# Turning attention scores over in 32x32 blocks on VectorE instead of by products with the identity on TensorE

## The chip, the cores and the metric

The kernel runs on one core of one Trainium2 chip. The metric is the device time of one execution in microseconds (us). Engines are named as the profile names them: PE is TensorE's matrix products, PEld its weight loads, DVE is VectorE, ACT is ScalarE, POOL is GpSimd, and SP issues the transfers (DMA).

## What is computed

Eight batches, each with eight heads, of 512 tokens and 32 state rows, 64 numbers a head, go through two softmaxes over one matrix of scores, and all rows then go through a feed-forward layer with a rational function between its two products:

```
scores = scale * np.matmul(x, state.transpose(0, 1, 3, 2))
a      = softmax over the last axis (the 32 state rows)
xread  = np.matmul(a, state)
scores2 = scale * np.matmul(state, x.transpose(0, 1, 3, 2))
a2     = softmax over the last axis (the 512 tokens)
sread  = np.matmul(a2, x)
h = concat(xread, sread) @ w_in
P = a0 + a1*h + a2*h^2 + a3*h^3
Q = 1 + |b0|*|h| + |b1|*h^2
out = (P / (Q + 1e-6)) @ w_out
```

`scores2` is `scores` transposed, so one set of products gives both. The weights are 512x2048 and 2048x512; they arrive as 64-bit numbers, and the kernel itself makes 32-bit ones of them.

## The kernel before, in words

**Front and back.** The work is 72 steps: batch b (0 to 7) has steps 8b to 8b+7, one for each eighth of the 2048 inner columns, and steps 64 to 71 do the same for the rows of `sread`. Step n begins with a *front* (`F:n:0` and `F:n:1`, line 687): 12 products of 128x512 that give 1024 columns of h in PSUM. xread is not formed: the state rows are multiplied with w_in once at the start (`X:i`, line 606, copied out by `XA:i` at line 618 and stored to DRAM) and the front multiplies that product (tile m) with the softmax weights (tile aT), both split into a high and a low part. ACT and DVE then make the rational function of h: ACT copies and logarithm and exponential (lines 699 to 802), DVE six operations of 128x1024 (`mu`, `po`, `qd`, `g1`, `g2`, `g3` at lines 710, 714, 720, 731, 737, 743), POOL the low part `gl` (line 750). The *back* (`mh:n:t` four products, `ml:n:t` two, line 760) multiplies them with w_out into four PSUM banks, one for each 128 tokens.

**Softmax of a batch.** It is done beside the steps of the batch ahead. `scores:b` (line 404) puts the scores into PSUM as ps_sc: partition 32k+s is state row s of head pair k, 2x512 columns are tokens. ACT copies them to sT (`sc_copy`). `row_T` turns sT over by eight 128x128 products with the identity (line 434, function `transposes`) into ps_s; DVE takes the maximum of each group of 32 (`row_max`, line 458) and subtracts it (`row_sub`, line 466), both from PSUM, into e1; ACT takes the exponential, DVE the sum, POOL multiplies with its reciprocal (`row_norm`, line 507). `a_T` turns e1 back by eight more products into ps_a; ACT takes its high part (`a_hi`, line 517), DVE the low part (`a_lo`, line 521). These are aT, which the fronts of the batch read. The other softmax runs along the columns of sT; its weights e2 are turned over by eight products of the same kind (`e2_T`).

**Buffers.** Four PSUM banks hold the outputs (o0 to o3), the other four are two buffers of the tag "h", which fronts, the products X and, from batch 1 on, ps_sc, ps_s, ps_a, ps_e and ps_sr take in turns. Batch 0 uses the output banks for its softmax.

**Order.** The program is a written list of 2266 operations (`ORDER`); each engine does its own instructions in the list's order and waits at each until its inputs are there and its output's buffer is free. SP issues all transfers in the list's order as well.

Of the kernel before, what the change touches and what calls it, by code (L numbers as in the profile page):

```python
# [18 lines left out]
P = 128  # L19
# [4 lines left out]
    "warm:8 lt:0:0 lr:0 cp:0 ls:0:2 scores:0:0 lr:1 jr:0 cp:1 jl:0 lc cb lt:0:1 scores:0:1 sc_copy:0:0 "  # L24
    "col_max:0:0 sc_copy:0:1 col_max:0:1 col_scale:0:0 lr:2 cp:2 X:0 fh:0 XA:0 col_scale:0:1 "
    "col_exp:0:1 lr:3 row_T:0:1 row_max:0:1 ls:2:8 row_sub:0:1 jw:0 XS:0 jr:1 X:3 fo:0 row_T:0:0 "
    "col_exp:0:0 X:1 row_exp:0:1 row_sum:0:1 lr:4 row_max:0:0 lr:5 XA:3 XS:3 cp:3 XA:1 row_sub:0:0 XS:1 "
    "e2_T:0:0 e2_copy:0:0 X:2 row_exp:0:0 lr:6 row_eps:0:1 row_norv:0:1 jl:1 a_T:0:1 row_sum:0:0 "
    "row_eps:0:0 a_hi:0:1 cp:4 XA:2 XS:2 e2_T:0:1 lr:7 X:5 row_norv:0:0 e2_copy:0:1 a_T:0:0 a_lo:0:1 "
    "col_eps:0 a_hi:0:0 a_lo:0:0 XA:5 XS:5 X:4 fh:1 cp:6 F:0:1 lq:0:0 fo:1 F:0:0 cp:5 jr:2 jl:2 b0a "  # L30
    "jr:3 XA:4 FC:0 lq:0:1 FB:0 qd:0 F:1:1 cp:7 F:1:0 lr:9 FB:1 FC:1 jl:3 XS:4 sp:7 sp:6 mu:0 po:0 qa:0 "
    "ln:0 qd:1 ex:0 jw:1 X:9 XA:9 lr:8 cp:8 lr:11 mu:1 po:1 lr:10 cp:10 XS:9 sread:0:0 cp:9 X:8 XA:8 "
    "XS:8 col_norm:0 jr:5 jr:4 jl:4 X:6 fh:2 fo:2 sread:0:1 sr_copy:0 g1:0 g2:0 XA:6 cp:11 lr:13 XS:6 "
    "qa:1 lr:15 sr_T:0 sr_fin:0 lr:14 jl:5 lr:12 g3:0 gl:0 X:12 fh:3 XA:12 XS:12 F:2:1 F:2:0 FC:2 FB:2 "
    "fo:3 sp:10 mh:0:0 mu:2 X:13 XA:13 XS:13 ln:1 sp:11 cp:12 qd:2 ex:1 mh:0:1 ml:0:1 cp:14 mh:0:2 "
    "ml:0:2 po:2 g1:1 g2:1 X:7 XA:7 jr:6 X:10 XA:10 ml:0:0 jr:7 cp:15 jl:7 lt:1:1 g3:1 gl:1 cp:13 qa:2 "
    "ln:2 X:11 XS:7 F:3:1 F:3:0 FB:3 FC:3 XA:11 jl:6 mh:0:3 ml:0:3 mh:1:3 ex:2 lt:1:0 scores:1:0 "
    "scores:1:1 XS:10 mu:3 qd:3 po:3 sp:14 sp:15 ml:1:3 lr:16 sc_copy:1 cp:16 lr:17 jw:4 mh:1:0 "
    "col_max:1 qa:3 lr:21 XS:11 X:17 X:14 XA:17 jw:2 jr:8 ml:1:0 g1:2 g2:2 g3:2 cp:17 ml:1:2 "
    "col_scale:1 XA:14 lr:20 X:15 XS:17 mh:1:2 row_T:1 row_max:1 row_sub:1 ln:3 mh:2:1 XS:14 jl:8 jw:3 "  # L40
    "cp:20 XA:15 XS:15 col_exp:1:0 cp:21 X:16 XA:16 lr:18 col_exp:1:1 gl:2 XS:16 lr:19 col_eps:1 fh:4 "
    "fo:4 X:18 XA:18 XS:18 row_exp:1 mh:1:1 cp:18 jr:10 jl:10 ml:1:1 X:20 fh:5 XA:20 fo:5 cp:19 F:4:1 "
    "F:4:0 FB:4 jr:9 col_norm:1 jl:9 X:21 FC:4 mh:2:2 mu:4 qd:4 sp:18 mh:2:3 XA:21 ml:2:1 sp:19 mh:2:0 "
    "lr:25 ex:3 ml:2:3 po:4 lr:22 XS:20 cp:22 g1:3 lr:23 cp:23 lr:24 cp:24 jr:12 XS:21 X:19 XA:19 XS:19 "
    "X:23 XA:23 cp:25 jr:11 jl:11 qa:4 lr:26 g2:3 g3:3 ml:2:0 sp:23 jl:12 X:22 sp:22 F:5:1 F:5:0 XS:23 "
    "FB:5 FC:5 mh:3:0 ml:2:2 mu:5 po:5 XA:22 cp:26 qd:5 lr:27 ln:4 mh:3:2 mh:3:1 XS:22 X:24 ex:4 g1:4 "
    "XA:24 XS:24 fh:6 fo:6 lm:8 mh:3:3 gl:3 lq:1:1 qa:5 ml:3:3 ml:3:0 X:26 XA:26 XS:26 ml:3:2 g2:4 g3:4 "
    "e2_T:1 e2_copy:1 row_sum:1 jr:13 cp:27 gl:4 X:25 XA:25 X:28 row_eps:1 row_norm:1:1 XS:25 jl:13 "
    "jw:7 mh:4:0 ln:5 ex:5 fh:7 F:6:1 XA:28 fo:7 g1:5 row_norm:1:0 F:6:0 FC:6 FB:6 qd:6 fs:8 ml:4:0 "
    "sp:26 ml:4:3 sp:27 XS:28 X:27 XA:27 lr:30 cp:30 ml:3:1 mu:6 po:6 qa:6 ln:6 ml:4:1 mh:4:2 lq:1:0 "  # L50
    "mh:4:3 X:30 XA:30 sread:1:0 sread:1:1 sr_copy:1 lr:28 g2:5 g3:5 gl:5 ex:6 mh:5:1 lr:31 mh:4:1 "
    "sr_T:1 sr_fin:1 cp:31 XS:27 XS:30 lr:29 X:29 XA:29 X:31 XA:31 mh:5:0 a_T:1 F:7:0 jr:15 F:7:1 jl:15 "
    "cp:28 ml:5:2 sp:31 mh:5:2 ml:5:3 g1:6 g2:6 a_hi:1 ml:4:2 a_lo:1 F:8:0 F:8:1 ml:5:1 sp:30 jr:14 "
    "cp:29 ml:5:0 FC:7 FB:7 mh:5:3 jl:14 qd:7 sp:29 sp:28 mh:6:3 mh:6:2 mu:7 po:7 mh:6:0 mh:6:1 lm:9 "
    "fs:9 FB:8 qd:8 qa:7 g3:6 F:9:1 F:9:0 gl:6 ml:6:2 ml:6:3 ln:7 ex:7 g1:7 mh:7:1 mh:7:2 FC:8 mu:8 "
    "po:8 FC:9 lm:10 ml:6:1 fs:10 FB:9 mh:7:3 F:10:1 g2:7 qa:8 ln:8 ex:8 F:10:0 g3:7 gl:7 ml:7:0 lm:11 "
    "ml:7:2 ml:7:1 qd:9 qa:9 ml:6:0 mu:9 po:9 FC:10 lm:13 lt:2:0 g1:8 FB:10 g2:8 g3:8 lt:2:1 scores:2:0 "
    "scores:2:1 mh:7:0 fl:7:2 gl:8 mu:10 po:10 qd:10 sc_copy:2 col_max:2 lq:2:1 ml:7:3 fl:7:3 mh:8:2 "
    "fl:7:1 fs:11 mh:8:3 mh:8:1 ml:8:1 ln:9 ml:8:3 ex:9 row_T:2 F:11:0 g1:9 g2:9 fl:7:0 mh:8:0 ml:8:0 "
    "mh:9:1 g3:9 row_max:2 F:11:1 mh:9:2 ml:8:2 mh:9:3 row_sub:2 qa:10 ln:10 ex:10 gl:9 ml:9:3 lm:12 "  # L60
    "ml:9:2 fs:12 F:12:0 FB:11 qd:11 qa:11 F:12:1 col_scale:2 col_exp:2:0 lm:16 g1:10 mh:10:1 ml:9:0 "
    "g2:10 g3:10 gl:10 mh:10:0 mh:9:0 FC:11 mu:11 po:11 ml:10:3 ml:10:1 fs:13 FB:12 ml:9:1 qd:12 "
    "col_exp:2:1 F:13:0 F:13:1 ln:11 ml:10:0 mh:10:2 ex:11 g1:11 mh:11:1 mh:11:3 mh:11:2 FC:12 FB:13 "
    "lq:2:0 g2:11 g3:11 FC:13 mh:10:3 gl:11 ml:11:1 mu:12 mh:11:0 po:12 lm:14 qd:13 ml:11:3 mu:13 po:13 "
    "row_exp:2 row_sum:2 qa:12 row_eps:2 e2_T:2 fd:7:1 fs:14 lm:15 fs:15 F:14:0 F:14:1 ln:12 ex:12 "
    "g1:12 mh:12:3 fd:7:2 fd:7:3 qa:13 ln:13 ex:13 mh:12:1 col_eps:2 col_norm:2 ml:11:0 ml:10:2 g2:12 "
    "g3:12 gl:12 mh:12:2 FC:14 g1:13 e2_copy:2 FB:14 qd:14 sread:2:0 sread:2:1 mh:13:1 jw:5 "
    "row_norm:2:1 sr_copy:2 sr_T:2 mu:14 row_norm:2:0 XS:29 sr_fin:2 po:14 g2:13 g3:13 mh:12:0 ml:12:0 "
    "ml:12:3 qa:14 ln:14 ex:14 lm:17 mh:13:0 g1:14 a_T:2 a_hi:2 fs:16 F:15:1 F:15:0 mh:13:2 ml:12:2 "
    "ml:11:2 a_lo:2 F:16:1 F:16:0 FC:15 ml:12:1 gl:13 ml:13:0 ml:13:3 ml:13:2 g2:14 FB:15 qd:15 mh:13:3 "  # L70
    "mu:15 po:15 mh:14:0 fd:7:0 fs:17 F:17:0 F:17:1 lt:3:0 g3:14 gl:14 qa:15 ln:15 mh:14:3 ml:13:1 "
# [860 lines left out]
```

## Time and profile before

| | |
|---|---|
| median of the runs | 690.88 us |
| lowest of the runs | 688.37 us |
| profiled execution, its own time | 690.54 us |
| its span in the trace | 688.7 us |
| busy in the span: PE, DVE, ACT, POOL | 661.9, 620.1, 524.1, 298.7 us |
| mean granted clock of TensorE | 0.987 |

A busy time is the time in which the engine had an instruction under way, also when that instruction itself was held up. Products are pipelined, so the cost of one is read from the distance of starts and not from its duration. "L434" is line 434 of the kernel before; in the changed kernel the lines behind the list stand a few numbers higher.

### The profile page before, as it was taken

Reading aid. Unit: us, or ns where it says so; the run is one execution under the profiler, and the core shown is the slowest. Engines: PE = TensorE matmul, PEld = TensorE weight load, DVE = VectorE, ACT = ScalarE, POOL = GpSimd, SP = SyncE. Lnnn points to the kernel's source line nnn. Section 1 sums busy time; section 2 is a strip of 40 time slices with the busy share of each in tenths; the row PEclk is TensorE's granted clock in tenths of the full one; section 3 lists DMA queues with packets and bytes.
Section 4 is the critical chain, followed back from the end, with each engine's and each line's share of the span. In section 5 each row is a group of like instructions: output and inputs, shape, how many; then the busy total and the mean of one; then the engine's idle time right before and its main releaser. Section 6 shows DMA issues by size and latency. Waiting matters only on the chain.

```text
span 688.7 us, 11564 instructions
## 1 busy us (share of the span) xinstructions
PE 661.9 (96%) x4602; PEld 525.3 (76%) x4602; DVE 620.1 (90%) x589; ACT 524.1 (76%) x641; POOL 298.7 (43%) x172
## 2 busy tenths in 40 slices
PE   6688889999999999999999999999999999999997
PEld 4455556778887778878887888788878788888895
DVE  4788689999999999999999999999899889998996
ACT  5889789887876876877778677777887777666773
POOL 0024146554554454434554444354444445445542
PEclk8989999999999999999999999999999999999999
DMA  7988877605122300451015022221203021300311
GB/s 290 327 298 327 304 290 277 225 37 196 64 77 92 127 17 25 125 190 39 18 60 199 15 98 72 92 82 71 78 33 137 2 75 55 99 0 33 107 47 30
DMA packets 29434, 81.49 MB, mean 118 GB/s; under 512 B 3268, under 2 KB 3396, under 8 KB 29380
## 3 DMA queue, kind: packets, MB, share of 16 engines
q1 hardware_dynamic: 29380, 80.75, 33.8%
q8 instruction: 36, 0.59, 0.4%
q14 instruction: 18, 0.15, 0.1%
HBM read 52.95 MB, written 27.79 MB: 117 GB/s over the span
## 4 chain that ended last, share of the span: by engine, by line
PE 77%; DVE 7%; DMA 6%; ACT 5%; issue 2%; POOL 1%; SPq 0%; POOLq 0%; ACTq 0%; DVEq 0%
PE h L687 25%; DMA m_dram<-xo 3%; DMA raw<-in_w_in_dram 2%; ACT xo L618 2%; PE o__3063 L760 2%; PE ps_x L606 2%; PE o__5992 L760 2%; PE o__3659 L760 2%; PE o__4266 L760 2%; PE o__3652 L760 2%; PE o__3604 L760 2%; PE o__5977 L760 2%; PE o__5430 L760 2%; PE o__3107 L760 2%; PE o__4244 L760 2%
## 5 line engine op out<-in xcount | busy, mean ns | idle before, releaser
L750 POOL TENSOR_TENSOR gl<-C,L 128x1024 fp32r<-128x1024 f32 (+1 forms) x71 | 168.9, 2379 | 271.1 <-DVE C L743 170.0
L687 PE MATMUL h<-aT,m 128*128 128x512 f32 x768 | 188.6, 392 | 0.8 <-ACT xo L618 0.8
L687 PEld LDWEIGHTS h<-aT,m 128*128 128x128 f32 x768 | 143.1, 188 | 33.1 <-ACT xo L618 2.9
L699 ACT ACTIVATE C<-h,cst 128x1024 f32<-128x1024 f32 (+1 forms) x72 | 83.1, 1156 | 40.9 <-PE h L687 33.3
L706 ACT ACTIVATE A<-h,cst 128x1024 f32<-128x1024 f32 (+1 forms) x72 | 76.9, 1068 | 47.1 <-PE h L687 41.7
L731 DVE SCALAR_TENSOR_TENSOR gh<-C,cst,L 128x1024 fp32r<-128x1024 f32 (+1 forms) x72 | 95.6, 1328 | 13.1 <-ACT L L802 9.5
L720 DVE SCALAR_TENSOR_TENSOR A<-A,b0a,h 128x1024 f32<-128x1024 f32 (+1 forms) x72 | 87.4, 1214 | 14.2 <-ACT A L706 10.4
L647 POOL TENSOR_TENSOR m<-m_sb,m 128x512 fp32r<-128x512 f32 x56 | 75.0, 1348 | 46.1 <-ACT m L646 22.0
L743 DVE SCALAR_TENSOR_TENSOR C<-C,cst,A 128x1024 f32<-128x1024 f32 (+1 forms) x72 | 91.0, 1263 | 2.1
L714 DVE SCALAR_TENSOR_TENSOR C<-C,cst,h 128x1024 f32<-128x1024 f32 (+1 forms) x72 | 87.7, 1219 | 1.9
L737 DVE SCALAR_TENSOR_TENSOR A<-A,gh 128x1024 f32<-128x1024 f32 (+1 forms) x72 | 87.5, 1216 | 1.7
L710 DVE TENSOR_TENSOR C<-C,h 128x1024 f32<-128x1024 f32 (+1 forms) x72 | 83.0, 1154 | 5.3 <-ACT C L699 2.7
L726 ACT ACTIVATE A<-A 128x1024 f32<-128x1024 f32 (+1 forms) x72 | 72.7, 1012 | 15.4 <-DVE A L720 15.4
L792 ACT ACTIVATE L<-A 128x1024 f32<-128x1024 f32 (+1 forms) x72 | 73.0, 1015 | 3.4 <-POOL gl L750 0.5
L802 ACT ACTIVATE L<-L 128x1024 f32<-128x1024 f32 (+1 forms) x72 | 73.1, 1015 | 1.8
L606 PE MATMUL ps_x<-win_sb,st 64*32 64x256 f32 x1024 | 39.6, 432 | 12.3 <-ACT xo L618 6.1
L337 POOL TENSOR_TENSOR wo<-cv_r,wo 128x512 fp32r<-128x512 f32 x16 | 23.3, 1476 | 59.8 <-ACT wo L336 59.6
L606 PEld LDWEIGHTS ps_x<-win_sb,st 64*32 64x32 f32 x1024 | 18.5, 116 | 28.1 <-issue 10.8
L646 ACT CAST m<-m_sb 128x512 fp32r<-128x512 f32 x56 | 33.9, 615 | 2.9 <-PE h L687 2.9
L618 ACT COPY xo<-ps_x 128x1024 f32<-128x1024 f32 (+1 forms) x32 | 28.8, 908 | 5.3 <-DMA m_dram<-xo 4.1
L299 ACT ACTIVATE cv_y<-raw 128x512 f32<-128x512 f32 x32 | 21.9, 695 | 11.1 <-DMA raw<-in_w_in_dram 8.7
L687 PEld LDWEIGHTS h<-sh,m 128*128 128x128 f32 x192 | 24.1, 191 | 0.6
(266 smaller groups left out, 1124.0 us busy)
## 6 DMA issues: line engine op xcount, KB each, us to landing
m_sb<-m_dram SPq DMA_DIRECT2D x56, 256.0 KB, 3.7
m_dram<-xo SPq DMA_DIRECT2D x24, 512.0 KB, 4.6
out_dram<-o_sb SPq DMA_DIRECT2D x34, 256.0 KB, 3.3
xT_sb<-in_xT_dram SPq DMA_DIRECT2D x16, 512.0 KB, 5.0
raw<-in_w_in_dram SPq DMA_DIRECT2D x16, 512.0 KB, 6.8
raw<-in_w_out_dram SPq DMA_DIRECT2D x16, 512.0 KB, 6.0
x_sb<-in_x_dram SPq DMA_DIRECT2D x16, 512.0 KB, 5.0
w_in_dram<-win_sb SPq DMA_DIRECT2D x8, 512.0 KB, 4.2
```

The costliest lines, as they stand in the source:

```text
L647: nc.gpsimd.tensor_tensor(m[:, 1], t, m[:, 0].bitcast(F32), op=ALU.subtract)
L687: nc.tensor.matmul(h[:, ci * W : (ci + 1) * W], l, r, start=(q == 0), stop=(q == len(seq) - 1),)
L699: nc.scalar.activation(e["C"], e["h"], AF.Identity, scale=cst[:, 3:4], bias=cst[:, 2:3])
L706: nc.scalar.activation(e["A"], e["h"], AF.Abs, scale=cst[:, 5:6])
L710: nc.vector.tensor_tensor(e["C"], e["C"], e["h"], op=ALU.mult)
L714: nc.vector.scalar_tensor_tensor(e["C"], e["C"], cst[:, 1:2], e["h"], op0=ALU.add, op1=ALU.mult)
L720: nc.vector.scalar_tensor_tensor(e["A"], e["A"], b0a, e["h"], op0=ALU.add, op1=ALU.mult)
L731: nc.vector.scalar_tensor_tensor(e["gh"], e["C"], cst[:, 0:1], e["L"], op0=ALU.add, op1=ALU.mult)
L737: nc.vector.scalar_tensor_tensor(e["A"], e["A"], 1.0 + 1e-6, e["gh"].bitcast(F32), op0=ALU.add, op1=ALU.mult)
L743: nc.vector.scalar_tensor_tensor(e["C"], e["C"], cst[:, 0:1], e["A"], op0=ALU.add, op1=ALU.subtract)
L750: eng.tensor_tensor(e["gl"], e["C"], e["L"], op=ALU.mult)
L760: nc.tensor.matmul(O[t], e[l][:, j * W + t * P : j * W + (t + 1) * P], wo[:, k, 2 * u + j, :], start=(place == FIRST[n // U, t] and i + j ...
```

## The change

`row_T` no longer uses TensorE: one DVE instruction turns over each 32x32 block of ps_sc on its way from PSUM to e1. A group of 32 state rows is a block's height, so each token's scores of one head again stand in 32 neighbouring columns, and `row_max` and `row_sub` work on e1 in SBUF. `a_T` is a DVE instruction of the same kind from e1 to a new tile eT, which for batches 1 to 7 lies in the buffer of e2; `a_hi` and `a_lo` read eT. `e2_T` keeps its products. `row_sub` is done by POOL in all batches (`row_sup`), `a_lo` by POOL in batches 0, 2, 3 and 4 (`a_lp`). Of the work at the start, five of the 32 copies `XA` go from ACT to DVE (`XV`) and four of the 16 weight splits from POOL to DVE (`sv`); one `row_norm` half and one 128x512 `gl` go from POOL to DVE as well. The list has the same length and is in another order throughout.

```diff
     def row_T(b, j=None):
-        transposes(b, "ps_s", 2, TS[b]["sT"], j)
+        e1 = once(b, "e1", at_tile("e1", [P, 2, S]))
+        for i in (0, 1) if b == 0 and j is None else (j,):
+            nc.vector.transpose(flat(half(e1, i)), flat(half(TS[b]["ps"], i)))
...
-            stat(mx, j), slots(TS[b]["ps_s"], j), axis=AX.X, op=ALU.max
+            stat(mx, j), slots(TS[b]["e1"], j), axis=AX.X, op=ALU.max
...
-        nc.vector.tensor_tensor(
-            slots(e1, j),
-            slots(T["ps_s"], j),
+        (eng or nc.vector).tensor_tensor(
+            e1,
+            e1,
...
     def a_T(b, j=None):
-        transposes(b, "ps_a", 2, TS[b]["e1"], j)
+        t = once(b, "eT", lambda: at.tile([P, 2, S], F32, name="eT", tag="e2" if b else "e2T"))
+        nc.vector.transpose(flat(half(t, j)), flat(half(TS[b]["e1"], j)))
...
-        nc.scalar.copy(half(AT[b][:, 0], j), half(TS[b]["ps_a"], j))
+        (copy or nc.scalar.copy)(half(AT[b][:, 0], j), half(TS[b]["eT"], j))
...
-        nc.vector.tensor_tensor(
+        (eng or nc.vector).tensor_tensor(
             half(a[:, 1], j),
-            half(TS[b]["ps_a"], j),
+            half(TS[b]["eT"], j),
...
+        "sv": lambda i: conv_split(i, nc.vector),
...
+        "a_lp": lambda b, j=None: a_lo(b, j, nc.gpsimd),
+        "row_sup": lambda b, j=None: row_sub(b, j, nc.gpsimd),
```

One line of the list on either side, out of batch 6:

```diff
-    "col_scale:6 ml:39:3 fl:39:2 FB:43 mh:40:2 ml:39:1 fl:39:0 lm:45 fl:39:3 row_T:6 mh:40:3 gl:40 "
+    "mh:41:1 FB:43 mh:41:0 g3:41 row_T:6 row_max:6 fl:39:2 fd:39:2 mh:40:2 ml:40:2 gl:41 ml:41:3 "
```

**TensorE, batch 6, between its scores and the end of its softmax.** Before (h is a front, o a back, ps_s the turned scores):

```order
L404 MATMUL ps_sc<-xT_sb,st 32x256 x16
L760 MATMUL o__3659<-wo,gl 128x512 x4
L687 MATMUL h<-aT,m 128x512 x12
L760 MATMUL o__3604<-wo,gl 128x512 x2
L760 MATMUL o__4244<-wo,gh 128x512 x4
L760 MATMUL o__3652<-wo,gl 128x512 x2
L434 MATMUL ps_s<-ident,sT 128x128 x8
L760 MATMUL o__4266<-wo,gh 128x512 x4
```

After, from the same scores on:

```order
L407 MATMUL ps_sc<-xT_sb,st 32x256 x16
L693 MATMUL h<-aT,m 128x512 x12
L766 MATMUL o__4177<-wo,gh 128x512 x4
L766 MATMUL o__4177<-wo,gl 128x512 x2
L766 MATMUL o__4177<-wo,gh 128x512 x4
L766 MATMUL o__4127<-wo,gh 128x512 x4
L766 MATMUL o__4204<-wo,gh 128x512 x4
```

The eight products with the identity are gone, here and where ps_a was made; the products around them are fronts and backs as before, in another order.

**VectorE, batch 6, the same place.** Before (mx is the row maximum, gh, A and C belong to the steps):

```order
L731 SCALAR_TENSOR_TENSOR gh<-C,cst,L 128x1024
L737 SCALAR_TENSOR_TENSOR A<-A,gh 128x1024
L743 SCALAR_TENSOR_TENSOR C<-C,cst,A 128x1024
L458 TENSOR_REDUCE mx<-ps_s 128x32
L466 TENSOR_TENSOR e_4378<-ps_s,mx 128x1024
L731 SCALAR_TENSOR_TENSOR gh<-C,cst,L 128x1024
```

After:

```order
L737 SCALAR_TENSOR_TENSOR gh<-C,cst,L 128x1024
L743 SCALAR_TENSOR_TENSOR A<-A,gh 128x1024
L749 SCALAR_TENSOR_TENSOR C<-C,cst,A 128x1024
L446 STREAM_TRANSPOSE e_4197<-ps_sc 128x1024
L463 TENSOR_REDUCE mx<-e_4197 128x32
L716 TENSOR_TENSOR C<-C,h 128x1024
```

A transpose of 128x1024 has come, and the subtraction has gone to POOL.

**GpSimd, batch 3 (after).** e_2363 is e1 of the batch; before, only the `gl`, the m splits and the two `row_norm` halves (L507 then, L512 now) stood there:

```order
L653 TENSOR_TENSOR m<-m_sb,m 128x512 x2
L471 TENSOR_TENSOR e_2363<-e_2363,mx 128x1024
L756 TENSOR_TENSOR gl<-C,L 128x1024
L653 TENSOR_TENSOR m<-m_sb,m 128x512
L756 TENSOR_TENSOR gl<-C,L 128x1024 x2
L653 TENSOR_TENSOR m<-m_sb,m 128x512
L512 TENSOR_TENSOR e_2363<-e_2363,rs 128x512 x2
L653 TENSOR_TENSOR m<-m_sb,m 128x512
L756 TENSOR_TENSOR gl<-C,L 128x1024 x2
L527 TENSOR_TENSOR aT<-eT,aT 128x1024
```

Two operations of 128x1024, the row subtraction (L471) and the low part of aT (L527), have come in between.

## Rows read from the trace of the kernel before

**Rows 1.** Busy time of the engines in four stretches of the span (columns: stretch in us, its length, then busy us of PE, PEld, DVE, ACT, POOL with their instructions, the granted clock of TensorE, the share of the DMA engines, GB/s).

```profile
0.00:103.00 103.00, 82.73 (x1103) 52.65 (x1103) 76.12 (x100) 80.81 (x116) 23.12 (x20) 0.92 0.85 307
103.00:137.70 34.70, 34.45 (x434) 24.45 (x434) 33.70 (x32) 31.51 (x44) 20.66 (x12) 1.00 0.71 249
137.70:620.00 482.30, 480.46 (x2697) 391.85 (x2696) 453.26 (x391) 368.80 (x425) 224.92 (x124) 1.00 0.23 78
620.00:688.70 68.70, 64.25 (x372) 56.34 (x371) 57.00 (x69) 42.97 (x60) 30.00 (x18) 1.00 0.17 55
```

**Rows 2.** Waits of PE from 103 to 620 us: who waited for whom, us in total, times, the longest.

```profile
PE o__4923 L760 <- POOL gl L750: 1.0, 1, 1.0
PE o__2418 L760 <- POOL gl L750: 0.5, 1, 0.5
PE o__1819 L760 <- POOL gl L750: 0.4, 1, 0.4
PE ps_sr L539 <- DVE C L714: 0.2, 1, 0.2
```

**Rows 3.** Timeline of PE around a `row_T` and an `a_T` of batch 7 (start us, duration us, engine, line, instruction, output and inputs, form, count), and at the end three groups of back products with nothing between them.

```profile
509.62 1.04 PE L434 MATMUL ps_s<-ident,sT 128*128 128x128 f32 x8
510.42 1.17 PE L760 MATMUL o__4244<-wo,gh 128*128 128x512 f32 x4
511.42 0.61 PE L760 MATMUL o__4284<-wo,gl 128*128 128x512 f32 x2
...
548.99 1.03 PE L434 MATMUL ps_a<-ident,e 128*128 128x128 f32 x8
549.78 0.72 PE L760 MATMUL o__4923<-wo,gl 128*128 128x512 f32 x2
...
542.25 1.07 PE L760 MATMUL o__4893<-wo,gh 128*128 128x512 f32 x4
543.15 1.07 PE L760 MATMUL o__4915<-wo,gh 128*128 128x512 f32 x4
544.06 1.07 PE L760 MATMUL o__4885<-wo,gh 128*128 128x512 f32 x4
```

**Rows 4.** Groups of instructions by line and form, of DVE, ACT and POOL (count, then busy us and mean ns of one, then the idle time before them and what ended it).

```profile
L458 DVE TENSOR_REDUCE mx<-ps_s 128x32 f32<-128x1024 f32 x7 | 8.5, 1218 | 1.3 <-PE ps_s L434 1.3
L466 DVE TENSOR_TENSOR e<-ps_s,mx 128x1024 f32<-128x1024 f32 x7 | 8.6, 1224 | 0.2
L521 DVE TENSOR_TENSOR aT<-ps_a,aT 128x1024 fp32r<-128x1024 f32 x7 | 8.5, 1217 | 1.4 <-ACT aT L517 1.4
L635 DVE TENSOR_TENSOR m<-ps_x,m 128x512 fp32r<-128x512 f32 x8 | 5.5, 686 | 2.9 <-ACT xo L618 1.9 <-ACT m L631 1.0
L309 DVE TENSOR_SCALAR cv_r<-raw 128x512 int32<-128x512 uint32 x32 | 15.6, 534 | 9.0 <-DMA raw<-in_w_in_dram 7.8 <-DMA raw<-in_w_out_dram 1.2
L618 ACT COPY xo<-ps_x 128x1024 f32<-128x1024 f32 x24 | 24.1, 1014 | 4.5 <-DMA m_dram<-xo 4.1 <-PE ps_x L606 0.4
L750 POOL TENSOR_TENSOR gl<-C,L 128x1024 fp32r<-128x1024 f32 x64 | 159.8, 2497 | 252.0 <-DVE C L743 154.9 <-PE h L687 20.2 <-ACT m L646 10.5
```

**Rows 5.** Waits of DVE from 103 to 620 us, the longest in total (columns as in rows 2).

```profile
DVE A L720 <- ACT A L706: 7.2, 10, 1.2
DVE gh L731 <- ACT L L802: 5.4, 9, 1.5
DVE A L720 <- ACT C L699: 3.6, 3, 2.3
DVE C L710 <- ACT C L699: 2.0, 5, 0.9
DVE aT L521 <- ACT aT L517: 1.4, 1, 1.4
```

**Rows 6.** Timeline of POOL and DVE at one place, and below it the two DVE lines whose two tensors both lie in SBUF and one that reads PSUM (duration of one in ns: least, median, most; first and last start; forms).

```profile
536.60 2.41 POOL L750 TENSOR_TENSOR gl<-C,L 128x1024 fp32r<-128x1024 f32 x1 [2.63 <-DVE C L743]
537.02 3.07 DVE L731 SCALAR_TENSOR_TENSOR gh<-C,cst,L 128x1024 fp32r<-128x1024 f32 x1 [0.59 <-ACT L L802]
540.02 1.21 DVE L710 TENSOR_TENSOR C<-C,h 128x1024 f32<-128x1024 f32 x1
...
L731 DVE SCALAR_TENSOR_TENSOR gh<-C,cst,L x72: 742/1280/3502, 43.8 to 679.5; 128x1024 fp32r<-128x1024 f32 x64, 128x512 fp32r<-128x512 f32 x8
L737 DVE SCALAR_TENSOR_TENSOR A<-A,gh x72: 682/1224/2202, 45.1 to 680.3; 128x1024 f32<-128x1024 f32 x64, 128x512 f32<-128x512 f32 x8
L710 DVE TENSOR_TENSOR C<-C,h x72: 674/1213/1224, 33.1 to 677.6; 128x1024 f32<-128x1024 f32 x64, 128x512 f32<-128x512 f32 x8
```

**Rows 7.** Groups of the three DVE lines with both tensors in SBUF, of 128x1024 (columns as in rows 4).

```profile
L731 DVE SCALAR_TENSOR_TENSOR gh<-C,cst,L 128x1024 fp32r<-128x1024 f32 x64 | 89.2, 1394 | 11.7 <-ACT L L802 8.7 <-PE o__5447 L760 1.2 <-PE o__2423 L760 0.7
L743 DVE SCALAR_TENSOR_TENSOR C<-C,cst,A 128x1024 f32<-128x1024 f32 x64 | 83.7, 1307 | 1.9
L737 DVE SCALAR_TENSOR_TENSOR A<-A,gh 128x1024 f32<-128x1024 f32 x64 | 82.0, 1281 | 1.4
```

**Rows 8.** The chain of waits (what ended last, followed back) from 0 to 103 us (shares of that stretch by line).

```profile
by line: DMA m_dram<-xo 15.3%; DMA raw<-in_w_in_dram 14.1%; ACT xo L618 11.7%; issue 8.6%; PE ps_x L606 7.0%; DMA xT_sb<-in_xT_dram 6.2%; PE h L687 5.9%; ACT cv_y L299 3.9%; ACT C L699 3.4%; DVE C L710 2.2%; ACT A L706 2.1%; ACT A L726 1.9%
```

More of the change, by code (lines that the diff above doesn't have):

```diff
@@ L330, in store_win, with conv_split @@
         nc.sync.dma_start(w_in32[u], win_t[u])
-    def conv_split(i):
+    def conv_split(i, eng):
         _, u, k = unit(i)
@@ L336, in conv_split @@
         nc.scalar.copy(wo[:, 0, f, :], m)
-        nc.gpsimd.tensor_tensor(
+        eng.tensor_tensor(
             wo[:, 1, f, :], m, wo[:, 0, f, :].bitcast(F32), op=ALU.subtract
@@ L367, in banks, with flat @@
         return ps_h.tile([P, 2, S], F32, name=name, tag="h")
+    def flat(t):
+        return t.rearrange("p j t -> p (j t)") if len(t.shape) == 3 else t
     def half(t, j):
@@ L458, in row_max, with row_sub @@
         nc.vector.tensor_reduce(
-            stat(mx, j), slots(TS[b]["ps_s"], j), axis=AX.X, op=ALU.max
+            stat(mx, j), slots(TS[b]["e1"], j), axis=AX.X, op=ALU.max
         )
-    def row_sub(b, j=None):
+    def row_sub(b, j=None, eng=None):
         T = TS[b]
-        e1 = once(b, "e1", at_tile("e1", [P, 2, S]))
+        e1 = slots(T["e1"], j)
         mx = stat(T["mx"], j)
-        nc.vector.tensor_tensor(
-            slots(e1, j),
-            slots(T["ps_s"], j),
+        (eng or nc.vector).tensor_tensor(
+            e1,
+            e1,
             mx.unsqueeze(2).broadcast_to([P, mx.shape[1], NS]),
@@ L511, in a_T, with a_hi, a_lo @@
     def a_T(b, j=None):
-        transposes(b, "ps_a", 2, TS[b]["e1"], j)
-    def a_hi(b, j=None):
+        t = once(b, "eT", lambda: at.tile([P, 2, S], F32, name="eT", tag="e2" if b else "e2T"))
+        nc.vector.transpose(flat(half(t, j)), flat(half(TS[b]["e1"], j)))
+    def a_hi(b, j=None, copy=None):
         if b not in AT:
             AT[b] = at.tile([P, 2, 2, S], F32R, name="aT", tag="aT", bufs=2)
-        nc.scalar.copy(half(AT[b][:, 0], j), half(TS[b]["ps_a"], j))
-    def a_lo(b, j=None):
+        (copy or nc.scalar.copy)(half(AT[b][:, 0], j), half(TS[b]["eT"], j))
+    def a_lo(b, j=None, eng=None):
         a = AT[b]
-        nc.vector.tensor_tensor(
+        (eng or nc.vector).tensor_tensor(
             half(a[:, 1], j),
-            half(TS[b]["ps_a"], j),
+            half(TS[b]["eT"], j),
             half(a[:, 0].bitcast(F32), j),
@@ L823, in attention_rational_ffn @@
         "jl": join_low,
-        "sp": conv_split,
+        "sp": lambda i: conv_split(i, nc.gpsimd),
+        "sv": lambda i: conv_split(i, nc.vector),
         "fh": fold_hi0,
```

324 rows, old and new, of the table ORDER are left out of this document.

## Prediction, made before the changed kernel ran

> **What bounds the kernel now.** I read the busy times by stretch first, then the waits of PE, then the timeline of PE. From 103 us to 620 us PE is busy 34.45 + 480.46 of 517.0 us at a granted clock of 1.00 [rows 1]; the reader is to see that only 2.1 us are left over, and that the waits explain them [rows 2]. Busy time alone could hide held-up products, so I looked at starts: four back products start 0.90 us apart from the next four, again and again [rows 3], which is 0.225 us each without a hole. So PE's own work sets the time from 103 us almost to the end, and whatever PE is spared there comes off the time, as long as the others keep up. DVE is the next: 486.96 of the same 517.0 us, 30 us idle [rows 1]. ACT and POOL have more room. The first 103 us are another regime: PE 82.7 us, DVE 76.1, ACT 80.8 us busy, DMA at 0.85 and 307 GB/s [rows 1], and the chain there runs over transfers of m and w_in, ACT's copies and their fronts [rows 8]. PE spared there saves next to nothing.
>
> **What the change takes from PE.** 128 products with the identity go. A group of eight stands from 509.62 to 510.42, and the back products behind it take 1.00 us for four (510.42 to 511.42) where 0.90 is usual: 0.80 + 0.10 = 0.90 us for the group; 548.99 to 549.78 gives 0.79 for the first part again [rows 3]. After 103 us there are 13 such groups: `row_T` of batches 2 to 7 and `a_T` of batches 1 to 7. 13 x 0.90 = **11.7 us** off the path. The three groups' worth ahead of that (batch 0, and `row_T` of batch 1) lie in the stretch that PE does not bound: nothing, at the most 3 x 0.9 = 2.7 us if PE were to bound there. Two of five softmax tiles also no longer take one of the two "h" buffers; that can give back part of the 2.1 us of PE's waits at best.
>
> **What it puts on DVE.** Fourteen transposes of 128x1024 and four of 128x512. The trace has no such operation. Nearest in shape and in where it reads is the reduction of 128x1024 from PSUM, 1.22 us [rows 4]; I take that, and 0.69 us for a half. From below, a one-input operation of 128x512 ran in 0.534 us [rows 4], so 1.07 us for 1024; from above, two passes over the data would be 2.4 us. In the stretch from 103 to 620 us: 13 transposes x 1.22 = +15.9; `row_sub` of six batches goes to POOL, -6 x 1.22 = -7.3; `a_lo` of three batches too, -3 x 1.22 = -3.7; three weight splits come, 3 x 0.69 = +2.1 [rows 4]. Together +7.0 us. [...]
>
> One more term: DVE's operations with both tensors in SBUF lose time to POOL. `gl` ran from 536.60 for 2.41 us, and a `g1` that started at 537.02 took 3.07 instead of 1.28 us, that is, it stood until `gl` ended; lines with a PSUM operand never went over 1.22 us [rows 6]. Over the run this cost (1394 - 1280) x 64 + (1281 - 1224) x 64 ns = 10.9 us [rows 6, 7], at 298.7 us of POOL. `row_sub` and `a_lo` on POOL add about ten operations of 2.4 us [rows 4], so 24 x 10.9 / 298.7 = 0.9 us more for DVE; the `a_lo` that stay on DVE now have both tensors in SBUF, at the same rate nothing to speak of. DVE then needs 486.96 + 7.0 + 0.9 = 494.9 us in a stretch of 517.0 - 11.7 = 505.3 us: 98% busy, 10.4 us of idle time where it had 30. It fits, but barely. DVE's waits are for ACT's A, L and C, at most 2.3 us each, and the named ones add up to 19.6 us [rows 5]; they arise because DVE is ahead of PE's fronts, and they shrink when it is not. Leads in the list are about as long as before: between the end of a front and its first back product stand other products of PE worth 82 of 512 columns on average before and 81 now, at the least 54 and 44.
>
> **The other parts.** ACT loses five copies of 1.01 us [rows 4], all at the start, DVE gains them at about 1.22 each: the start is bound by transfers, whose bytes ahead of step 5 are the same in both lists, so I take zero, from -5 us (ACT's share of the chain is returned) to +6 us (DVE, at 76 of 103 us, becomes late). `row_sub` on POOL lengthens the softmax's chain by 2.4 - 1.2 us; the scores stand tens of us ahead of the fronts that need them, which covers it. `a_lo` on POOL sits directly ahead of the front in three batches and behind `gl` in POOL's queue: 0 to 2.4 us each, I take 0. The new wait is that of `a_T` for the buffer of e2, so for PE's `e2_T`; behind it on DVE stand the six operations of a step, and PE would wait for those. The list puts `e2_T` ahead in each batch, so 0, with 0 to 1 us each as bound. SP's queue has the same 208 transfers.
>
> **Sum.** 690.54 (profiled execution; its span 688.7, the median of runs 690.88) - 11.7 + 0 = **679 us**.
>
> **Rivals.**
> - *The start shortens as well.* For it: the chain there holds ACT's copies with 11.7% [rows 8], and ACT gets 5 us back. Against it: the DMA share of 0.85 [rows 1]. 679 - 5 = 674 us.
> - *DVE becomes the bound of the long stretch.* If half of its 30 us of idle time stays, it needs 494.9 + 15 = 509.9 us, 4.6 more than PE: 684 us; with the waits for `e2_T` and POOL on top, up to 690.
> - *The lock.* If each of the ten new POOL operations holds a DVE operation for its whole length, DVE needs 494.9 + 24 = 519 us and sets the time: 519 - 505.3 = 13.7 us on top of 679, so 693 us: no gain. [...]
> - *Transposes at twice the price: slower.* At 2.4 us each, 13 x 1.2 = 15.6 us more: DVE needs 510.5, with 15 us of idle time 525.5 us, 8.5 more than the stretch takes today; the start, with five transposes and 6 us of copies more on DVE, loses another 6: 705 us. It decides from (517.0 - 15 - 494.9) / 13 + 1.22 = 1.77 us a transpose on that the gain is gone. [...]
>
> **Numbers.** Forecast as argued 0.56 (673 to 685), shorter start 0.18 (670 to 677), DVE the bound 0.14 (683 to 692), lock 0.05 (690 to 700), dear transposes 0.07 (698 to 712). The range 670 to 691 us leaves out most of the last two and a little at the low end. A measurement of this kernel tells 2% from no change, so faster means below 677.1 us, slower above 704.7. The forecast falls below 677.1 in about a third of its cases (0.19), the shorter start nearly always (0.17): faster 0.36; slower, from the dear transposes, 0.05; the rest, 0.59, is within 2%.
>
> **What would show it.** The transposes' rows: 1.2 us or not. PE still without holes after the start, and the stretch of 517 us shorter by about 12; PE's busy time near 650 us (661.9 - 11.7). DVE's near 636 us: 620.1 and 0.9 for the lock, +19.8 for all transposes, -14.9 for all `row_sub` and five of nine `a_lo` instructions, +10.3 for copies, splits and the two halves, by the same prices; its waits for ACT cut. PE becomes dense near 103 us as before. If instead PE shows waits for DVE or for POOL in the long stretch, the second or third rival holds. If DVE's two-SBUF lines have a mean well above 1.39 and 1.28 us, it is the lock. I am wrong if the start has moved by more than 5 us either way.

## The result and the profile after

The changed kernel takes **674.25 us** (median; 673.40 to 674.53) against 691.00 for the kernel before on the same chip: ratio 0.9768, 95% interval 0.9739 to 0.9797. One slow execution of the kernel before, 745.57 us, is left out of the ratio but is in the median of 691.00. The profiled execution took 673.98 us, its span is 672.2 us.

Busy time by stretch, cut as in [rows 1] except for the last stretch, with the same columns:

```profile
0.00:103.00 103.00, 79.52 (x1114) 49.77 (x1115) 88.01 (x105) 80.35 (x115) 32.59 (x25) 0.95 0.87 314
103.00:137.70 34.70, 33.74 (x401) 24.30 (x401) 33.16 (x39) 30.11 (x41) 13.50 (x8) 1.00 0.70 245
137.70:620.00 482.30, 482.30 (x2686) 394.83 (x2685) 467.26 (x406) 378.94 (x437) 253.14 (x136) 1.00 0.24 78
620.00:672.20 52.20, 47.74 (x278) 41.78 (x276) 42.40 (x57) 28.78 (x45) 18.13 (x13) 0.98 0.20 61
```

In the long stretch PE now has no gap at all (482.30 of 482.30), while DVE is busy 467.26 us of it, 97%, where it had 453.26. Both are nearly full at once.

Groups of DVE and POOL by line and form: the transposes, and what answers to [rows 4] and [rows 7].

```profile
L446 DVE STREAM_TRANSPOSE e<-ps_sc 128x1024 f32<-128x1024 f32 x7 | 8.7, 1242 | 0.0
L518 DVE STREAM_TRANSPOSE eT<-e 128x1024 f32<-128x1024 f32 x7 | 8.7, 1240 | 0.5 <-POOL m L653 0.3
L463 DVE TENSOR_REDUCE mx<-e 128x32 f32<-128x1024 f32 x7 | 8.5, 1219 | 0.2
L737 DVE SCALAR_TENSOR_TENSOR gh<-C,cst,L 128x1024 fp32r<-128x1024 f32 x64 | 89.3, 1396 | 2.8 <-ACT L L808 1.7
...
L471 POOL TENSOR_TENSOR e<-e,mx 128x1024 f32<-128x1024 f32 x7 | 13.4, 1920 | 0.3 <-DVE mx L463 0.3
L527 POOL TENSOR_TENSOR aT<-eT,aT 128x1024 fp32r<-128x1024 f32 x3 | 7.3, 2420 | 0.0
```

A transpose of 128x1024 takes 1.24 us, from PSUM and from SBUF alike. DVE's waits, 103 to 620 us, against [rows 5]:

```profile
DVE A L726 <- ACT A L712: 4.9, 10, 0.9
DVE gh L737 <- ACT L L808: 1.7, 3, 0.9
DVE C L716 <- ACT C L705: 1.5, 3, 0.6
```

The wait for L fell from 5.4 to 1.7 us. `a_T`'s new wait for `e2_T` does not show at all.

**Where the 16.5 us of the span came from.** Both traces hold the same 2592 products of fronts and backs, so I compared the start of the k-th in each. Around the 100th the two are level (82.4 us for 81.9; the 101st 82.7 for 83.3). The 200th starts 3.5 us earlier than before (119.1 for 122.6 us), the 300th 2.8, the 1000th 9.0, the 2000th (553.2 for 569.6) 16.4, the last 16.5. So some 3 us were won in the start, about 13 along the batches, and nothing after. The share of the start is the less certain one, since the old start itself varies: the kernel with `a_T` alone on DVE (below) is the kernel before up to its first transpose at 127.9 us, and its 200th product starts at 126.4 us. The fronts of the steps 64 to 71 show the same from their own rows (least, median, most; first and last start); before:

```profile
L687 PE MATMUL h<-sh,m x192: 274/283/283, 626.2 to 673.7; 128*128 128x256 f32 x192
```

After:

```profile
L693 PE MATMUL h<-sh,m x192: 274/283/283, 610.7 to 656.4; 128*128 128x256 f32 x192
```

### The profile page after: what moved, and what is told of

The parts are those of the page before. It is cut to its first block, busy times and chain, and to the rows that moved or that the text cites. A ratio compares the mean times of both kernels' runs of the same rounds, so it can differ in the third digit from the quotient of the medians.

```text
span 672.2 us, 11314 instructions
## 1 busy us (share of the span) xinstructions
PE 643.3 (96%) x4474; PEld 510.7 (76%) x4474; DVE 630.8 (94%) x604; ACT 518.2 (77%) x636; POOL 317.4 (47%) x180
## 4 chain that ended last, share of the span: by engine, by line
PE 86%; DMA 6%; DVE 4%; ACT 3%; issue 1%; SPq 0%; DVEq 0%; ACTq 0%
PE h L693 28%; DMA m_dram<-xo 4%; PE ps_x L612 2%; PE o__1774 L766 2%; PE o__4177 L766 2%; PE o__2967 L766 2%; PE o__3602 L766 2%; PE o__3569 L766 2%; PE o__1790 L766 2%; PE o__2927 L766 2%; PE o__2379 L766 2%; PE o__5870 L766 2%; PE o__3617 L766 2%; PE o__5292 L766 2%; PE o__1781 L766 2%; PE o__5875 L766 2%
## 5 line engine op out<-in xcount | busy, mean ns | idle before, releaser
L653 POOL TENSOR_TENSOR m<-m_sb,m 128x512 fp32r<-128x512 f32 x56 | 80.0, 1432 | 49.9 <-ACT m L652 30.8
L749 DVE SCALAR_TENSOR_TENSOR C<-C,cst,A 128x1024 f32<-128x1024 f32 (+1 forms) x72 | 89.0, 1236 | 2.0
L612 PE MATMUL ps_x<-win_sb,st 64*32 64x256 f32 x1024 | 35.9, 401 | 10.2 <-DVE C L720 3.9
L337 POOL TENSOR_TENSOR wo<-cv_r,wo 128x512 fp32r<-128x512 f32 x12 | 16.9, 1414 | 41.9 <-ACT wo L336 41.9
L624 ACT COPY xo<-ps_x 128x1024 f32<-128x1024 f32 (+1 forms) x27 | 23.7, 887 | 6.9 <-PE ps_x L612 3.1
L693 PE MATMUL h<-sh,m 128*128 128x256 f32 x192 | 24.7, 282 | 0.0
```

What stands on the lines that cost most here:

```text
L653: nc.gpsimd.tensor_tensor(m[:, 1], t, m[:, 0].bitcast(F32), op=ALU.subtract)
L693: nc.tensor.matmul(h[:, ci * W : (ci + 1) * W], l, r, start=(q == 0), stop=(q == len(seq) - 1),)
L749: nc.vector.scalar_tensor_tensor(e["C"], e["C"], cst[:, 0:1], e["A"], op0=ALU.add, op1=ALU.subtract)
```

## Experiments

The operations of the changed kernel were first put into the list of before, then parts of the change were undone or doubled, and last one transpose at a time was tried on the old list. In the kernels on the old list batch 0 keeps its products, and the start is that of before. "Ratio" is to the kernel before on the same chip, with its 95% interval.

### Both transposes on the list of before

```diff
 def row_T(b):  # batches 1 to 7
-    transposes(b, "ps_s", 2, sT)
+    nc.vector.transpose(e1, ps_sc)
 def a_T(b):
-    transposes(b, "ps_a", 2, e1)
+    nc.vector.transpose(eT, e1)
-ORDER: after's
+ORDER: before's (e2_T:7, e2_copy:7 ahead of a_T:7)
```

> The list of the kernel before, with the transposes of batches 1 to 7 on VectorE (row_sub and a_lo stay on VectorE, batch 0 keeps its products, e2_T of batch 7 stands ahead of its a_T because they share a buffer). Theory PE (PE's own work sets the time after the start, a group of eight products is worth 0.90 us): 691.0 - 13 x 0.90 = 679 us, 677 to 682, if VectorE keeps up, which needs 487 + 16 = 503 us of 505. Theory order (the gain came from the new list): 687 to 692. Theory VectorE (it is as much the bound as PE, the relief by GpSimd was needed): 684 to 695, with waits of PE for VectorE in the long stretch.

Measured: **707.42 us** (704.80 to 709.54), ratio 1.0263 (1.0233 to 1.0293): some 18 us slower than before, where every theory had less. The long stretch, columns as above:

```profile
137.70:620.00 482.30, 463.50 (x2534) 367.38 (x2535) 464.69 (x393) 360.08 (x416) 226.80 (x121) 1.00 0.22 78
```

DVE is no busier than in the changed kernel (464.69 against 467.26), and yet PE stands idle for 18.8 us. Totals do not tell these two apart. The groups of DVE show one reason:

```profile
L482 DVE TENSOR_TENSOR e<-e,mx 128x1024 f32<-128x1024 f32 x7 | 12.6, 1795 | 0.2
L542 DVE TENSOR_TENSOR aT<-eT,aT 128x1024 fp32r<-128x1024 f32 x7 | 11.8, 1687 | 4.0 <-ACT aT L538 4.0
```

`row_sub` and `a_lo` now have both tensors in SBUF and take 1795 and 1687 ns instead of 1224 and 1217 [rows 4]: 7 x (571 + 470) ns = 7.3 us more, and `a_lo` waits 4.0 us for ACT's copy.

With these subtractions on POOL, as in the change (`row_sub` of batches 1 to 7, `a_lo` of 2 to 4):

```diff
-    row_sub:b ... a_lo:b
+    row_sup:b ... a_lp:b
```

> As the run before, and row_sub of batches 1 to 7 and a_lo of batches 2 to 4 on GpSimd as in the changed kernel. Theory PE: 679 us, 677 to 681, the same as without GpSimd; what is left to the 674.3 us of the changed kernel is the new list's own share, some 5 us. Theory order: 687 to 692. Theory VectorE: 4 us or more below the run without GpSimd.

Measured: **716.70 us** (714.88 to 717.08), ratio 1.0394 (1.0374 to 1.0414): worse still, and outside every expectation. The trace puts 7.0 us on PE's fronts waiting for POOL's low part of aT:

```profile
PE h L708 <- POOL aT L542: 7.0, 3, 3.0
PE o__3544 L781 <- POOL gl L771: 3.6, 1, 3.6
```

What helps in the changed list hurts in this one, since in batches 2 to 4 `a_lo` stands there right ahead of the batch's first front; in the changed list 6, 26 and 3 operations stand between.

### Products back, on the new list

`a_T` of batches 1 to 7 by products, in the changed list; since the turned weights take a buffer of the fronts again, `a_T`, `a_hi` and `a_lo` were put side by side, `a_lo` on DVE:

```diff
-    a_T:4 ... a_hi:4 ... a_lp:4      # apart, a_T on DVE
+    a_T:4 a_hi:4 a_lo:4              # together, a_T on PE
```

> The changed kernel and its list, with a_T of batches 1 to 7 done by eight products with the identity again (a_lo of these batches on VectorE, a_T, a_hi and a_lo side by side, 8.7 us of transposes less on VectorE and 3.7 us of a_lo more). Theory PE: 674.3 + 7 x 0.90 = 680.6 us, 679 to 683. Theory order: 674 to 676. Theory VectorE: 672 to 675, since VectorE has 5 us less to do.

Measured: **698.54 us** (697.48 to 700.68), ratio 1.0146 (1.0121 to 1.0171), above every expectation. DVE stands 17.3 us, six times, for ACT's copy that it used to find ready:

```profile
DVE aT L538 <- ACT aT L534: 17.3, 6, 4.6
DVE A L737 <- ACT C L716: 10.9, 6, 4.8
```

So this run measures my placing more than the products. The gentler half is `row_T` of batches 2 to 7 by products, `row_sub` back on DVE directly behind `row_max`, all else as in the change:

```diff
 def row_T(b):
+    if b > 1:
+        transposes(b, "ps_s", 2, sT)
+        return
-    row_T:4 row_max:4 row_sup:4
+    row_T:4 row_max:4 row_sub:4
```

> The changed kernel with row_T of batches 2 to 7 by products with the identity again and row_sub of these batches on VectorE, reading PSUM, right behind row_max; a_T stays a VectorE transpose and everything else stands as in the changed list. VectorE loses six transposes (6 x 1.24) and gets six subtractions (6 x 1.22): no load more or less; GpSimd is spared 6 x 1.92 us. PE gets six groups of products. Theory 'PE' (the products' own time is the whole price): 674 + 6 x 0.72 to 0.90 = 678 to 680. Theory 'places' (VectorE's queue now has a wait for PE's products and the subtraction some operations earlier than the list meant, and the turned scores take one of the two buffers of the fronts): over 682, with PE waiting for VectorE in the long stretch. Under 677 would say that row_T's products cost nothing on this list.

Measured: **686.17 us** (684.78 to 687.70), ratio 0.9944 (0.9923 to 0.9965), 11.9 us above the change. Theory "places" had over 682, but with PE waiting for DVE, and that is not where the wait shows. DVE waits for PE:

```profile
DVE mx L473 <- PE ps_s L444: 13.8, 6, 4.8
```

With a product in the place of a transpose DVE waits 2.3 us on average, at most 4.8, for a result that comes through another queue. In the trace of before DVE mostly comes to `row_max` after the products, and this wait was 1.3 us in all [rows 4]. As an estimate, six groups at 0.87 us (measured below), 5.2, and 58 to 70% of the 13.8 us of DVE's time (below as well), 8.0 to 9.7, make 13.2 to 14.9 us, a little over the 11.9; the run does not separate the two.

### The prices, on the new list

Twice the products of `e2_T` in batches 1 to 7 (56 more):

```diff
 def e2_T(b, j=None):
-    transposes(b, "ps_e2", 0, e2, j)
+    for _ in range(2 if b else 1):
+        transposes(b, "ps_e2", 0, e2, j)
```

> The changed kernel with the eight products of e2_T made twice in batches 1 to 7, same tile, same output: 56 products more on PE, nothing more on any other engine. Theory PE: 674.3 + 7 x 0.90 = 680.6 us, 679.5 to 682. Theory VectorE (co-bound): 674 to 677.

Measured: **679.27 us** (677.52 to 680.23), ratio 0.9853 (0.9832 to 0.9874): 5.0 us for seven groups, 0.72 each, nearly theory PE. (By the ratios to the kernel before, which ran at 689.15 us on this chip, it is 5.9 us, 0.84 each.) The traces give the price on PE itself. In the change:

```profile
251.09 1.04 PE L437 MATMUL ps_e<-ident,e 128*128 128x128 f32 x8
251.88 0.71 PE L766 MATMUL o__2427<-wo,gl 128*128 128x512 f32 x2
```

With the products made twice:

```profile
251.93 1.91 PE L437 MATMUL ps_e<-ident,e 128*128 128x128 f32 x16
253.59 0.71 PE L767 MATMUL o__2443<-wo,gl 128*128 128x512 f32 x2
```

From the group's start to that of the next product it is 0.79 us for eight and 1.66 us for sixteen: 0.87 us for the eight added. By the count of fronts and backs the 300th product starts at 146.2 us in both kernels and the 2500th 5.5 us later (656.7 for 651.2); six of the added groups lie between, 5.2 us of PE's time. PE stays without a gap (482.30 of 482.30 us). So in the long stretch its own time is the price; the group of batch 1, at 104 us, cost nothing.

`row_sub` and `a_lo` from POOL back to DVE (batches 1 to 7, and 2 to 4):

```diff
-    row_sup:b ... a_lp:b
+    row_sub:b ... a_lo:b
```

> The changed kernel and its list with row_sub of batches 1 to 7 and a_lo of batches 2 to 4 back on VectorE: ten operations of 1.22 us, 12.2 us more for VectorE, whose idle time between 137.7 and 620 us is 482.3 - 467.3 = 15.0 us. Theory PE (VectorE has room as long as its work fits): 674 to 677 us. Theory VectorE: 680 to 686 us.

Measured: **682.36 us** (681.80 to 682.47), ratio 0.9881 (0.9854 to 0.9908), 8.1 us above the change, as theory VectorE had. Its trace gives the subtractions 1421 and 1344 ns, 14.0 us in all, so 58% of the time given to DVE came through.

Each transpose of batches 1 to 7 done twice (14 x 1.24 = 17.4 us more):

```diff
-    nc.vector.transpose(...)
+    for _ in range(2 if b else 1):
+        nc.vector.transpose(...)
```

> The changed kernel with each transpose of batches 1 to 7 made twice, as if it cost 2.48 us: 14 x 1.24 = 17.4 us more for VectorE, which is about its idle time in the long stretch (15.0 us). Theory PE with VectorE close behind: some of it comes through, 678 to 686 us, and PE shows holes that VectorE's lines end. Theory VectorE (the bound already): 689 to 692 us, all of it. If it is 674 to 676, VectorE has more room than its busy time tells.

Measured: **686.37 us** (683.91 to 689.00), ratio 0.9933 (0.9906 to 0.9960), 12.1 us above the change: 70% came through, the upper end of "PE with VectorE close behind". The long stretch has PE at 474.96 of 482.30 us. So in the changed kernel both engines bind: what PE gets in the long stretch shows in full (5.5 us for 5.2), and of what DVE gets 58 to 70%.

The five copies `XV` back on ACT (`XA`), nothing else:

```diff
-    XV:18
+    XA:18
```

> The changed kernel with the five copies of the start (XV) back on ScalarE: 5 us more for ScalarE and 6 us less for VectorE, all ahead of 103 us. Theory A (the start was shortened by ScalarE's relief): 676.5 to 680 us. Theory B (the start is set by transfers, or by VectorE): 672 to 675 us.

Measured: **679.44 us** (678.75 to 680.17), ratio 0.9840 (0.9813 to 0.9868): 5.2 us lost, as theory A had. By the same count as above, the 100th product is 1.9 us late, the 200th 4.8, and 4.8 it stays to the 2500th. The traces say why, in PE's waits from 0 to 103 us. In the kernel before:

```profile
PE ps_x L606 <- ACT xo L618: 6.1, 4, 2.7
```

In this run, with the copies on ACT:

```profile
PE ps_x L619 <- ACT xo L631: 4.8, 3, 2.3
PE ps_x L619 <- DVE C L727: 4.7, 3, 3.0
```

In the changed kernel, where the wait of ps_x for ACT's copy is 0.7 us:

```profile
PE ps_x L612 <- DVE C L720: 3.9, 2, 3.0
PE ps_x L612 <- DVE win_sb L325: 3.0, 3, 1.4
PE h L693 <- DVE xo L624: 1.9, 2, 1.1
```

The products X wait for a buffer that ACT's copy has to empty; the DMA share of 0.85 hid that from me. The granted clock of the first 103 us is 0.95 with the copies on either engine, so these 5 us are not the clock's; before had 0.92 there, and what that is worth in the start was not separated. The wait for `win_sb`, one of the weight conversions, is not among those of before. At one place (POOL, then DVE) it is the lock of [rows 6] again:

```profile
73.67 2.40 POOL L756 TENSOR_TENSOR gl<-C,L 128x1024 fp32r<-128x1024 f32 x1 [8.55 <-DVE C L749]
73.78 3.37 DVE L325 SCALAR_TENSOR_TENSOR win_sb<-cv_y,cv_r 128x1024 int32<-128x1024 int32 x1 [0.28 <-ACT cv_y L299]
```

Both tensors of this `win_sb` lie in SBUF, and it takes 3.37 us where the median of the eight is 1.23, ending at 77.15, 1.08 us after `gl`; the `gh` of [rows 6] also ended 1.08 us after its `gl` (540.09 and 539.01). So the new start also loses time to the order of POOL and DVE.

### One thing at a time, on the old list

Only `row_T` of batches 1 to 7 on DVE, the products of `a_T` kept:

```diff
 def row_T(b):  # kernel before, batches 1 to 7
-    transposes(b, "ps_s", 2, sT)
+    nc.vector.transpose(e1, ps_sc)
```

> The list of before, with row_T of batches 1 to 7 as a VectorE transpose (row_max and row_sub then read SBUF, both on VectorE) and a_T by products with the identity as before. PE is spared 7 x 0.90 = 6.3 us, VectorE gets 7 x 1.24 = 8.7 us and loses about 4 us more where row_sub, now with both tensors in SBUF, meets GpSimd (1795 instead of 1224 ns in the run with both transposes on the old list). Theory 'room' (before's list leaves VectorE no room at the places where the softmax stands, so added VectorE time comes through in full and what PE is spared is worth nothing): 691 + 12.7 = 700 to 706. Theory 'round trip' (the loss on the old list comes from a_T, whose result VectorE's a_lo waits for by way of ACT's a_hi, with the steps behind it in the queue): little here, 687 to 694. Theory 'totals' (PE is the bound until VectorE is full): 685 to 688.

Measured: **698.88 us** (698.47 to 700.34), ratio 1.0110 (1.0084 to 1.0135), 7.5 us slower, just under "room" and well over the others. One place in the timeline shows how the time is lost (POOL, DVE and then PE):

```profile
240.36 1.21 DVE L474 TENSOR_REDUCE mx<-e 128x32 f32<-128x1024 f32 x1
240.58 2.40 POOL L771 TENSOR_TENSOR gl<-C,L 128x1024 fp32r<-128x1024 f32 x1 [1.23 <-DVE C L764]
241.60 2.46 DVE L482 TENSOR_TENSOR e<-e,mx 128x1024 f32<-128x1024 f32 x1
...
247.63 1.21 PE L781 MATMUL o__2407<-wo,gh 128*128 128x512 f32 x4 [1.58 <-DVE gh L752]
```

The step's last operation C has just released `gl` on POOL, `row_sub` is next but one on DVE and now reads two tensors from SBUF: it takes 2.46 us instead of 1.22 and ends at 244.06, again 1.08 us after `gl` (242.98), which I read as standing until `gl` ends; the back products further on wait 1.58 us for `gh`. It is the lock of [rows 6], at a place where the old list often brings the two together: the mean of the seven is 1797 ns. In before, `row_sub` read PSUM and took 1224 ns [rows 4].

Only `a_T` on DVE, the products of `row_T` kept (`e2_T:7` and `e2_copy:7` again ahead of `a_T:7`):

```diff
 def a_T(b):  # kernel before, batches 1 to 7
-    transposes(b, "ps_a", 2, e1)
+    nc.vector.transpose(eT, e1)
```

> The list of before, with a_T of batches 1 to 7 as a VectorE transpose (a_hi and a_lo read SBUF, a_lo on VectorE) and row_T by products as before. PE is spared 6.3 us, VectorE gets 8.7 us and about 3.3 us of lost time in a_lo, now with both tensors in SBUF (1687 instead of 1217 ns). Theory 'room': 691 + 12 = 700 to 705. Theory 'round trip': nearly the whole loss of both transposes on this list (16 to 18 us) is here, 702 to 708, and VectorE's a_lo waits for ACT's a_hi by over 5 us in total. Theory 'totals': 685 to 688.

Measured: **696.93 us** (693.99 to 700.21), ratio 1.0079 (1.0053 to 1.0105), 5.6 us slower, between the expectations. `a_lo` took 1641 ns and waited 3.3 us for ACT, under the 5 us of "round trip". The two halves together lose 13.1 us, both at once some 18: no single transpose carries the loss.

The kernel before with 14 x 1.22 = 17.1 us more on DVE at the same places, and nothing else:

```diff
 def row_max(b, j=None):  # and a_lo alike
-    nc.vector.tensor_reduce(...)
+    for _ in range(2 if b else 1):
+        nc.vector.tensor_reduce(...)
```

> The kernel before with its products, its list and its tiles, but row_max and a_lo of batches 1 to 7 done twice, one behind the other: 14 x 1.22 = 17.1 us more for VectorE at the places where the transposes would stand, nothing taken from PE, no new wait and no two-SBUF operand. Theory 'room': the 17.1 us come through nearly in full, 704 to 709. Theory 'round trip': what cost the time on the old list were the transposes' waits, so the load alone is partly covered by VectorE's 30 us of idle time, 692 to 699. Theory 'totals': VectorE needs 487 + 17 = 504 of 517 us, PE stays the bound, 691 to 693.

Measured: **696.28 us** (695.95 to 696.85), ratio 1.0069 (1.0046 to 1.0092): 4.9 us for 17.1, 29%, within the range of "round trip". The old list does have room for DVE work, so theory "room" falls. Load is not what costs most there: with 12.7 us of DVE time and 6.3 us *less* on PE, `row_T` alone cost more than 17.1 us of plain load. That the lock and the later results behind it make the difference is argued from the place above; no run takes the lock away alone.

Last, the old list with only the chain of the row softmax moved to the places it has in the new list:

```diff
-    mu:27 po:27 qd:27 row_T:4 row_max:4 row_sub:4 mh:24:0
+    g3:25 row_T:4 row_max:4 row_sub:4 gl:25
```

> Both transposes of batches 1 to 7 on VectorE, row_sub and a_lo on VectorE, the list of before for everything but the chain of the row softmax (row_T, row_max, row_sub, exponential, sum, normalisation, a_T, a_hi, a_lo): these stand behind the same operations of the steps as in the changed kernel's list, as far as their inputs allow. Theory 'places' (where these operations stand is what the new list gives): near the changed list with the same operations on VectorE, which took 682.4 us, and the 3 us of its shorter start more, so 683 to 689. Theory 'whole list' (the order of the steps' own operations carries it, and moving the softmax alone does nothing): 701 to 710. In between, 690 to 700, says that both share it.

Measured: **736.51 us** (731.65 to 738.07), ratio 1.0638 (1.0594 to 1.0682), outside every expectation. The granted clock of the long stretch is 0.96, where before and the change have 1.00; how much of the 45.2 us goes with it was not separated. PE's fronts wait for `a_lo` and DVE for ACT:

```profile
PE h L707 <- DVE aT L541: 9.6, 4, 4.9
...
DVE A L740 <- ACT A L726: 14.8, 10, 6.0
DVE rs L509 <- ACT e L505: 7.0, 4, 3.1
```

So these places alone, as far as the inputs allowed to carry them over, do not make the new list. Almost the same operations, both transposes and the subtractions on DVE, took 682.36 us in the new list, 707.42 in the old and 736.51 in the mixture. The first of them also has batch 0's transposes and the new start, which is worth 3.5 to 5.2 us; the rest of the 25 and 54 us goes with the order.

## Why the prediction was right, and where it was not

The forecast of 679 us in a range of 670 to 691 held; the result lies 4.75 us under it. By its steps:

- **PE sets the long stretch: right.** It is now busy without a gap there, and added products cost their own time. The price of 0.90 us a group holds: an added group of e2_T took 0.87 us on PE, so the 13 groups are worth 11.3 us (9.4 at the 0.72 of the medians). With the waits of PE that went (480.46 of 482.30 us busy before, 482.30 after: 1.8 us) that makes 13.1; about 13 were counted along the batches.
- **The start taken as zero: wrong.** It gave some 3.5 us between the two traces. The bound of -5 was there, and it is the first rival, with its 674 us, that hit the figure. The term failed because I took the share of the transfers as the limit; what PE waited for most was ACT's copy of a buffer, 6.1 us. Undoing the five copies costs 5.2 us, more than the start gained in all, so the other edits there cost something; `win_sb` behind POOL is a candidate, not tested.
- **Transposes at 1.22 us: right**, 1.24 measured, the choice by the nearest row and not by the bounds. The rival of dear transposes falls. The reduction of the same size, which was the price taken, still runs in 1.22 us beside them.
- **"It fits, but barely": right in the total**, DVE 97% busy in the long stretch for the 98% forecast. But DVE is then a second bound, not slack: 58 to 70% of what it is given shows. The subtractions on POOL were worth 8.1 us. On POOL `row_sub` took 1.92 us instead of 2.4.
- **The list costed at nothing: wrong, and the largest error of the argument.** I had compared one mean, the leads of 82 and 81, and called them equal. Of the three orders that ran with both transposes on DVE, only the new one earns anything. On the old list the same exchange loses some 18 us, one transpose of the two 5.6 to 7.5. That the list's zero did no harm to the sum was luck as far as the argument goes: equal leads were its only reason, and they say nothing of the lock or of where `a_lo` stands.
- **The lock:** 0.9 us more was forecast; `gh` and A cost (1396 - 1280) x 64 + (1276 - 1224) x 64 ns = 10.8 us, as before (10.9); the start's `win_sb` is outside this sum. In the changed kernel the rival falls. The prediction's "never went over 1.22 us" for lines with a PSUM operand does not hold for lines 714 and 720, which read h from PSUM too and have means of 1278 and 1273 ns in before. They go no higher than 1282 ns, also where they start beside a running `gl` with over 1 us of it left (23 times on line 714 and 12 on line 720 in 128x1024, from 100 to 680 us of before), so the reading that the lock spares them stands. On the old list the lock shows (1797 ns for 1224), since there `row_sub` follows the operation that starts `gl`.
- **`a_lo` on POOL:** "directly ahead of the front" is how it stands in the old list; in the new one other operations stand between, and PE shows no wait for it. The 0 was right, though the place was misread.
- **Busy times:** PE 643.3 for 650, DVE 630.8 for 636. A busy time counts held-up instructions too, which may be why PE's fell by more than the work (18.6 us for 11.7).

Open: how the losses on the old list divide between the lock, the wait of `a_lo` for ACT and the later `gl`; whether an old order mended at a few places would do as well as the new one; and what the new order is worth with all products left on PE, since they were only put back one half at a time. None of these was tried. From 103 to 620 us an order alone could give back at most the 2.1 us that PE waited [rows 2], for PE's own work fills the rest.

## What to carry to other kernels

Where the in-order queues of two engines are nearly full (here 97 and 100%), price an exchange between them with the order it comes in: a sum of busy times did not give the time here, where almost the same operations took 682.36 us in one order and 707.42 in another. Before moving an operand from PSUM to SBUF, ask which operations thereby get two SBUF operands, and what GpSimd starts just then (`row_sub` went from 1224 to 1797 ns on the old list). At a start with a high DMA share (here 0.85), still read PE's waits: the longest in total here, 6.1 us, was for a copy that empties PE's buffer.

## What the runs showed of the hardware

- A 32x32-block transpose of 128x1024 32-bit numbers takes 1.24 us on DVE, whether it reads PSUM or SBUF; of 128x512, 0.70 to 0.72 us. Neighbouring reductions of the same size take 1.22.
- POOL's subtraction of a row value that is repeated over 32 columns takes 1.92 us, that of two full tensors 2.42 us.
- Eight 128x128 products with the identity, added to a group in a dense stream, took 0.87 us more of PE from start to start (1.66 for 0.79); the medians rose by 0.72 us a group.
- A DVE operation with both tensors in SBUF stood beside a POOL operation of 2.40 us for 2.46 us instead of 1.22 (`row_sub`), and for 3.37 instead of 1.23 (`win_sb`), and ended 1.08 us after it both times.
